# Two gated linear-attention blocks on one core: the ten sums of transposed x move from VectorE to GpSimd

## The chip, the core and the metric

The kernel runs on one core of a Trainium2 chip. A core has five engines with a queue of their own: TensorE (PE, with its weight loads shown as PEld), VectorE (DVE), ScalarE (ACT), GpSimd (POOL) and SyncE (SP), which here only issues DMAs. The metric is the device time of one execution in microseconds (us). The kernel before took 175.12 us, the median of three runs (174.89, 175.12, 175.48).

## What is computed

Two linear-attention blocks, A and B, read the same x (2048 x 640, bf16) and have their own weights. A gate mixes their results.

```python
H, Dh = 32, 20
qkv = x @ wqkv                       # 2048 x 1920, split into q, k, v
phi = lambda t: where(t > 0, t + 1, exp(t)) + 1e-6
kv = sum over s of phi(k)[s] v[s]^T  # per head, 20 x 20
z  = sum over s of phi(k)[s]         # per head, 20
o  = (phi(q) @ kv) / (phi(q) . z + 1e-6)
a, b = (o @ wo) of block A, of block B
g = sigmoid((x * gate_w).sum(-1))
out = g * a + (1 - g) * b
```

## The kernel before, in words

x stands in SBUF twice: as it is (`XN`, 16 tiles of 128 rows) and transposed (`XT`, five chunks of 128 features by 2048 rows). Tiles 0 and 1 are transposed by TensorE, the others by DMA transposes on SP's queue: tiles 2, 3, 4 and 5 alone, then 6 and 7, then 8 to 11, then 12 to 15.

The work has stages that follow one another on TensorE. First, phi(k) of both blocks for all 16 row tiles (stage K, tokens that begin with K in the list `MAIN`). Then G, products of phi(k) with x, from which k^T v is had without computing v. Then Q and R, phi(q) for the four blocks of 512 rows; small products that make one matrix per block out of kv and wo; and O, the output.

Many of these products of 2 x 2 blocks are made with seven block products in place of eight (a Strassen scheme): sums and differences of the operands are formed first, seven products are taken, and the results are combined. In stage K this is done for two pairs of row tiles, `KU = (3, 6,)`: unit 3 is x tiles 6 and 7, unit 6 is x tiles 12 and 13. Its functions:

- `kw_sums` forms four sums of the weights (`KW[1]` to `KW[4]`, lines about 774), on VectorE, once.
- `kx_sums(u)` forms five differences of transposed x for unit u: `KX[u, 1]` to `KX[u, 4]` have 128 partitions x 256 columns, `KX[u, 5]` has 128 x 128, all bf16. That is line 795, and there are ten in all. `KX[u, 2]` needs `KX[u, 1]`, and `KX[u, 4]` needs `KX[u, 2]`. All five need the two transposed tiles.
- `ks_unit(u)` holds the seven products (line 823 on TensorE). In the order of `MAIN` they are K3.1, K3.2, K3.5, K3.6, K3.7, K3.3, K3.4, with products of other tiles between them. Step 5 reads `KX[u, 1]`, step 6 `KX[u, 2]`, step 7 `KX[u, 3]`, and step 3 reads `KX[u, 4]` and `KX[u, 5]`. ScalarE saves two of the products (line 829), and VectorE adds them to others (lines 834 and 836).

Behind every k product, `k_post` makes phi: ScalarE takes the exponential (line 706) and the relu (lines 718, 733) out of PSUM, VectorE clamps the exponential (line 709) and adds the two (lines 724, 736), or does relu and sum in one (line 745). A two-bank piece of PSUM becomes free when these have read it, and TensorE can't begin the next product before that; there are eight banks. VectorE also forms the sums of phi(k) for stage G (`s_pair`, line 895) and of x (`t_all`, line 920). Later, the line 1003, 1029 sums serve stage Q, lines 1219 and 1233 stage G. GpSimd does some memsets at the start, four broadcasts of the gate (line 985) and the padding of wv (line 550).

The order on each engine is fixed before the run. The order of TensorE is written out by hand in `MAIN`. For the other engines, the class `Sched` plans: every operation has an engine, an assumed cost, the buffers it reads and writes, and a priority, and the planner takes on each engine the operation that can start first by these assumed costs, at equal start the one of lower priority number. The assumed costs have no other effect. What results is one queue for each engine, with semaphore waits where an operation needs another engine's (or an earlier own) result.

Of the kernel before, what the change touches and what calls it, by code (L numbers as in the profile page):

```python
# [113 lines left out]
class Sched:  # L114
# [9 lines left out]
    def op(self, eng, fn, cost, ins=(), outs=(), after=(), prio=None, name="", dma=None):  # L124
        if eng == "ACT" and dma is None:
            after = list(after) + self.consts
        o = Op(eng, fn, cost, list(ins), list(outs), after, (self.base or len(self.ops)) if prio is None else prio, name, dma)
        self.ops.append(o)
        return o
# [184 lines left out]
def body(nc, A_x, A_wqkv, A_wo, B_x, B_wqkv, B_wo, gate_w, out, log=None):  # L314
# [153 lines left out]
    def dve2(n):  # L468
        return 150 + 0.53 * n
# [312 lines left out]
    def kx_sums(u):  # L782
        t1, t2 = 256 * u, 256 * u + 128
        a11, a12, a21, a22 = [XT[:, c : c + 2, lo : lo + 128] for lo in (t1, t2) for c in (0, 2)]
        for k, in0, in1, need in (
            (1, a21, a22, ()),
            (2, a11, KX[u, 1], (1,)),
            (5, XT[:, 4, t1 : t1 + 128], XT[:, 4, t2 : t2 + 128], ()),
            (3, a21, a11, ()),
            (4, a12, KX[u, 2], (2,)),  # L790
        ):
            bkx[u, k] = Buf("kx")
            op(
                "DVE",
                lambda e, k=k, in0=in0, in1=in1: e.tensor_tensor(out=KX[u, k], in0=in0, in1=in1, op=ALU.subtract),
                dve2(128 if k == 5 else 256),
                ins=[bxt[2 * u], bxt[2 * u + 1]] + [bkx[u, j] for j in need],
                outs=[bkx[u, k]],
                name="kx",
            )  # L800
# [156 lines left out]
    for t in range(2, KT):  # L957
        k_both(t, "AB" if t in RELUB else "A")
        if t % 2:
            s_pair(t // 2)  # L960
        if t == KWT:
            kw_sums()
        for u in KU:
            if t == KXT[u]:
                kx_sums(u)
# [802 lines left out]
```

## Time and profile before

| | |
|---|---|
| median of three runs | 175.12 us |
| the profiled execution | 175.57 us |
| its span (first to last instruction) | 174.1 us |
| TensorE clock granted | 1.00 |
| busy: PE, DVE, ACT, POOL | 170.8, 142.5, 115.9, 4.9 us |
| stage K on TensorE | 3.75 to 47.3 us |
| stage G begins | 47.4 us |
| line 795, ten sums, 128x256 each 0.28 us, 128x128 each 0.22 us | five from 20.15 us, five from 30.08 us |

The page of the profile gives for each engine the busy time and its share of the span. The waits list who was idle and what ended it. The timeline lists instructions in order of their start: start in us, time in us, engine, line of the kernel, operation, output<-inputs, shapes, and, where several like ones follow one another, how many were merged. A queue's own row (SPq, ACTq) is the issue of a DMA, and the landing is told apart. Matmul ends are modelled, so a busy PE may still have small holes; the starts show them.

### The profile page before, as it was taken

Reading aid. Unit: us, or ns where it says so; the run is one execution under the profiler, and the core shown is the slowest. Engines: PE = TensorE matmul, PEld = TensorE weight load, DVE = VectorE, ACT = ScalarE, POOL = GpSimd, SP = SyncE. Lnnn points to the kernel's source line nnn. Section 1 sums busy time; section 2 is a strip of 40 time slices with the busy share of each in tenths; the row PEclk is TensorE's granted clock in tenths of the full one; section 3 lists DMA queues with packets and bytes.
Section 4 is the critical chain, followed back from the end, with each engine's and each line's share of the span. In section 5 each row is a group of like instructions: output and inputs, shape, how many; then the busy total and the mean of one; then the engine's idle time right before and its main releaser. Section 6 shows DMA issues by size and latency. Waiting matters only on the chain.

```text
span 174.1 us, 3381 instructions
## 1 busy us (share of the span) xinstructions
PE 170.8 (98%) x1327; PEld 107.3 (62%) x1327; DVE 142.5 (82%) x262; ACT 115.9 (67%) x225; POOL 4.9 (3%) x17
## 2 busy tenths in 40 slices
PE   9899999999999999999999999999999999999995
PEld 4455555555577776766555565655556677777773
DVE  2187999999999946948879989799999994999441
ACT  5369999999963323145998895766899773556423
POOL 2000000000000061000000000000000000000000
PEclk9999999999999999999999999999999999999999
DMA  6979999990000025329920003376842012460035
GB/s 185 302 146 152 203 324 367 357 223 18 4 0 0 0 41 98 75 49 188 235 65 0 4 2 62 76 204 150 269 114 82 0 38 79 92 218 4 0 111 191
DMA packets 33036, 20.59 MB, mean 118 GB/s; under 512 B 18261, under 2 KB 32893, under 8 KB 33021
## 3 DMA queue, kind: packets, MB, share of 16 engines
q1 hardware_dynamic: 32062, 19.76, 44.6%
q10 hardware_dynamic: 958, 0.63, 1.2%
q8 instruction: 10, 0.16, 0.4%
q14 instruction: 6, 0.04, 0.1%
HBM read 10.88 MB, written 4.26 MB: 87 GB/s over the span
## 4 chain that ended last, share of the span: by engine, by line
PE 96%; DMA 3%; SPq 0%; ACT 0%; issue 0%
PE ps L1184 22%; PE ps L1582 22%; PE ps L658 15%; PE ps L1056 13%; PE ps L1152 10%; PE ps L823 6%; PE ps L659 4%; DMA WKW<-in_A_wqkv_dram 3%; PE ps L1446 1%; PE ps L1372 1%; PE ps L1340 1%; SPq L451 0%; ACT PKS L1647 0%; PE ps L635 0%
## 5 line engine op out<-in xcount | busy, mean ns | idle before, releaser
L658 PE MATMUL ps<-WKW,XT 128*128 128x512 bf16 x120 | 33.9, 380 | 0.8 <-DMA WKW<-in_A_wqkv_dram 0.8
L659 PE MATMUL ps<-WKW,XT 128*128 128x128 bf16 (+1 forms) x120 | 26.3, 219 | 0.0
L1184 PE MATMUL ps<-TX,PKS 128*128 128x321 bf16 (+1 forms) x160 | 23.5, 300 | 0.0
L706 ACT ACTIVATE EKT<-ps 128x640 bf16<-128x640 f32 x30 | 20.8, 721 | 3.4 <-PE ps L659 3.0
L658 PEld LDWEIGHTS ps<-WKW,XT 128*128 128x128 bf16 x120 | 11.8, 98 | 15.1 <-DMA WKW<-in_A_wqkv_dram 1.1
L1184 PEld LDWEIGHTS ps<-TX,PKS 128*128 128x128 bf16 x160 | 15.6, 98 | 6.9 <-DVE DEN L1233 0.2
L1184 PE MATMUL ps<-XN,PKS 128*128 128x321 bf16 (+1 forms) x120 | 18.2, 300 | 0.0
L1184 PEld LDWEIGHTS ps<-XN,PKS 128*128 128x128 bf16 x120 | 11.7, 98 | 5.2
L895 DVE TENSOR_TENSOR PKS<-PKS 128x1280 bf16<-128x1280 bf16 (+2 forms) x20 | 12.9, 680 | 0.0
L718 ACT ACTIVATE PKS<-ps 128x640 bf16<-128x640 f32 x18 | 12.8, 724 | 0.0
L1214 ACT ACTIVATE EKT<-ps 128x321 f32<-128x321 f32 (+1 forms) x12 | 5.2, 438 | 11.2 <-PE ps L1184 5.6
L659 PEld LDWEIGHTS ps<-WKW,XT 128*128 128x128 bf16 x120 | 11.8, 98 | 0.0
L1088 ACT ACTIVATE EQ<-ps 128x512 bf16<-128x512 f32 x18 | 10.7, 604 | 1.5 <-PE ps L1056 1.0
L1163 ACT ACTIVATE EQ<-ps 128x1024 bf16<-128x1024 f32 x8 | 8.2, 1028 | 4.8 <-PE ps L1152 3.1
L709 DVE TENSOR_SCALAR EKT<-EKT 128x1280 bf16<-128x1280 bf16 (+1 forms) x20 | 8.2, 419 | 2.7 <-ACT EKT L706 2.7
L1056 PE MATMUL ps<-XT,WQA 128*128 128x512 bf16 x36 | 10.2, 379 | 0.0
L1065 ACT ACTIVATE PKS<-ps 128x512 f32<-128x512 f32 x12 | 7.0, 602 | 4.1 <-PE ps L1056 4.1
L1152 PE MATMUL ps<-XT,WQB 128*128 128x512 bf16 x40 | 9.4, 381 | 0.0
L1152 PE MATMUL ps<-XT,WQA 128*128 128x512 bf16 x40 | 9.3, 380 | 0.0
L1219 DVE TENSOR_TENSOR WKW<-ps,EKT 128x320 bf16<-128x320 f32 x12 | 5.8, 485 | 3.1 <-PE ps L1184 3.0
L724 DVE TENSOR_TENSOR PKS<-PKS,EKT 128x1280 bf16<-128x1280 bf16 x9 | 7.4, 817 | 0.1
L1605 DVE TENSOR_TENSOR PKS<-ps,EKT 128x320 bf16<-128x320 f32 x7 | 3.4, 491 | 4.7 <-PE ps L1582 2.7
(182 smaller groups left out, 338.7 us busy)
## 6 DMA issues: line engine op xcount, KB each, us to landing
out_dram<-PKS SPq DMA_DIRECT2D x15, 160.0 KB, 1.8
XN<-in_A_x_dram SPq DMA_DIRECT2D x1, 2240.0 KB, 9.5
WKW<-in_A_wqkv_dram SPq DMA_DIRECT2D x5, 160.0 KB, 4.3
WKW<-in_B_wqkv_dram SPq DMA_DIRECT2D x5, 160.0 KB, 4.1
WQA<-in_A_wqkv_dram SPq DMA_DIRECT2D x1, 800.0 KB, 11.1
WQB<-in_B_wqkv_dram SPq DMA_DIRECT2D x1, 800.0 KB, 12.3
WVA<-in_A_wqkv_dram SPq DMA_DIRECT2D x1, 800.0 KB, 12.4
PKS<-in_B_wqkv_dram SPq DMA_DIRECT2D x1, 800.0 KB, 5.0
```

Source lines behind the costliest of these rows:

```text
L658: e.matmul(a[:, 0:512], l, WK[X][:, c, 0:512], start=(c == 0), stop=(c == NC - 1))
L659: return e.matmul(a[:, 512:w], l, WK[X][:, c, 512:w], start=(c == 0), stop=(c == NC - 1))
L706: op("ACT", lambda e, i=i, ps=ps: e.activation(evg(i), psg(ps), ACT.Exp), act_cost(D), ins=[ps] + first, outs=[ek, b], name="ke")
L709: lambda e: e.tensor_scalar(EK[:, ek.slot : ek.slot + n, :], EK[:, ek.slot : ek.slot + n, :], 1.0, EPS, op0=ALU.min, op1=ALU.add),
L718: op("ACT", lambda e, X=X, ps=ps: e.activation(pkt(X, t), psg(ps), ACT.Relu), act_cost(D), ins=[ps], outs=[rk], name="kr")
L823: r = e.matmul(a[:, lo:hi], l, m[:, lo:hi], start=(first and i == 0), stop=(i == len(prs) - 1), skip_group_check=not first)
L895: lambda e: e.tensor_tensor(out=out, in0=a, in1=b, op=ALU.subtract),
L1056: r = e.matmul(PS[:, ps.slot, :], w, x, start=(first and i == 0), stop=(i == len(prs) - 1), skip_group_check=not first)
L1088: o = [op("ACT", lambda e: e.activation(EQ[:, eq.slot + h, :], pv(), ACT.Exp), act_cost(512), ins=ins, outs=[eq, ex], name="qe")]
L1152: r = e.matmul(PS[:, ps.slot + h, :], WQ[X][:, c, g::5], XT[:, c, 1024 + 512 * h : 1536 + 512 * h], start=(c == 0), stop=(c == NC - 1))
L1184: r = e.matmul(PS[:, ps.slot, 0:w], reg[:, j, :], mov(j, w), start=(first and j == 0), stop=(j == 7), skip_group_check=not first)
L1582: r = e.matmul(PS[:, ps.slot, 0:HALF], reg(g), mov(g), start=(first and g == 0), stop=(g == NC - 1), skip_group_check=not first)
```

## The change

In `kx_sums` the engine of the five differences is GpSimd ("POOL") in place of VectorE ("DVE"), and the assumed cost is 500 ns for 128 columns and 900 ns for 256, where the formula `dve2` gave 218 and 286 ns.

```diff
         ):
             bkx[u, k] = Buf("kx")
             op(
-                "DVE",
+                "POOL",
                 lambda e, k=k, in0=in0, in1=in1: e.tensor_tensor(out=KX[u, k], in0=in0, in1=in1, op=ALU.subtract),
-                dve2(128 if k == 5 else 256),
+                500.0 if k == 5 else 900.0,
                 ins=[bxt[2 * u], bxt[2 * u + 1]] + [bkx[u, j] for j in need],
                 outs=[bkx[u, k]],
                 name="kx",
```

Because the planner sees other costs and another engine, it lays out three queues anew. On GpSimd the ten differences stand behind the memsets of the start and ahead of line 985, in the order k = 1, 5, 2, 3, 4 for unit 3 and then the same for unit 6; the first waits for the DMA transpose of tiles 6 and 7, the sixth for that of tiles 12 to 15. On VectorE they are gone, and around their places line 895 sums come earlier (the fourth of the first four now ahead of line 834), line 836 comes directly behind line 834, and line 920 sums are grouped differently; up to about 62 us some line 895, 1003 and 1219 operations change places. On ScalarE one relu (line 733) stands two places later, and two exponentials (line 706) trade places with another. The orders of TensorE and of SP are the same instruction by instruction. TensorE's matmuls at K3.5, K3.6, K3.7 and K3.3 and their counterparts of unit 6 now wait for GpSimd's semaphore.

## The prediction

> **What bounds the kernel now.** I read the busy times of the page first, then the waits of PE, then the stages around the change, and last the single rows there.
>
> ```profile
> PE 170.8 (98%) x1327; PEld 107.3 (62%) x1327; DVE 142.5 (82%) x262; ACT 115.9 (67%) x225; POOL 4.9 (3%) x17
> ```
>
> PE computes for 170.8 of 174.1 us. The list of who waited for whom, for PE alone, says what is left:
>
> ```profile
> PE ps L658 <- DMA WKW<-in_A_wqkv_dram: 0.8, 1, 0.8
> PE ps L585 <- DVE ONE L483: 0.3, 1, 0.3
> ```
>
> Both waits are over at 5.34 us. Behind them PE runs without an idle time that the view counts; the only things I find in the timeline are 0.07 us before the matmul at 28.84 and about 0.1 us beyond an ordinary change of mode at 106.4. So what this change can save is at most some 0.2 us, and what it can lose is whatever makes PE wait. DVE decides that, as the busy times by stretch show (columns: PE, PEld, DVE, ACT, POOL, clock, DMA share, GB/s):
>
> ```profile
> 14.90:22.20 7.30, 7.30 (x56) 4.12 (x55) 7.16 (x15) 7.12 (x14) 0.00 (x0) 1.00 1.11 169
> 22.20:31.00 8.80, 8.80 (x66) 4.92 (x65) 8.62 (x18) 8.80 (x19) 0.00 (x0) 1.00 1.04 360
> 31.00:46.50 15.50, 15.50 (x116) 8.78 (x115) 15.33 (x26) 15.02 (x30) 0.00 (x0) 1.00 0.58 155
> 46.50:60.00 13.50, 13.50 (x101) 9.60 (x100) 13.38 (x26) 7.02 (x17) 0.00 (x0) 1.00 0.00 1
> ```
>
> From 15 to 60 us PE has no pause, and DVE is busy for 44.5 of the 45.1 us: two full engines side by side, PE just ahead as the bound. POOL does nothing there.
>
> **What is removed.** The ten sums stand in the view of line 795 and in DVE's timeline:
>
> ```profile
> L795 DVE TENSOR_TENSOR PQ<-XT x6: 215/280/284, 20.1 to 30.4; 128x256 bf16<-128x256 bf16 x4, 128x128 bf16<-128x128 bf16 x2
> L795 DVE TENSOR_TENSOR PQ<-XT,PQ x4: 281/282/285, 20.7 to 31.1; 128x256 bf16<-128x256 bf16 x4
> ...
> 20.15 0.62 DVE L795 TENSOR_TENSOR PQ<-XT 128x256 bf16<-128x256 bf16 x3
> 20.69 0.28 DVE L795 TENSOR_TENSOR PQ<-XT,PQ 128x256 bf16<-128x256 bf16 x1
> 20.89 0.81 DVE L895 TENSOR_TENSOR PKS<-PKS 128x1280 bf16<-128x1280 bf16 x1
> 21.62 0.28 DVE L795 TENSOR_TENSOR PQ<-XT,PQ 128x256 bf16<-128x256 bf16 x1
> ```
>
> From start to start the five sums of unit 3 hold DVE for 20.89 - 20.15 = 0.74 plus 21.83 - 21.62 = 0.21, together 0.95 us; those of unit 6 (30.08 to 30.82, 31.06 to 31.26) for 0.94 us. DVE is relieved of 1.9 us.
>
> **What GpSimd pays.** No row has a GpSimd sum of two tensors. The nearest is line 985, one input, also 128x256:
>
> ```profile
> L985 POOL TENSOR_SCALAR GSB<-GE x2: 842/1068/1293, 62.3 to 63.6; 128x256 bf16<-128x256 f32 x2
> L985 POOL TENSOR_SCALAR GSB<-GI x2: 842/842/842, 64.4 to 65.2; 128x256 bf16<-128x256 f32 x2
> ```
>
> Bounds for a 256-column sum: 0.28 us, DVE's own price (I have no row in which GpSimd beats DVE), and 1.68 us, the row twice, if the second input is read after the first. I take 0.84, the row itself, being the same engine and width; half, 0.42, for the two sums of 128 columns. A unit is 4 x 0.84 + 0.42 = 3.8 us.
> The Trainium skill ("GPSIMD Engine Reference", 3.1 Elementwise) gives 4.50 us for a two-input sum of 2048 fp32 columns; an estimate from it is 0.56 us for 256. With that the sum below would be 3.4 us in place of 4.7.
>
> **Is GpSimd in time?** Its queue takes them in the order k = 1, 5, 2, 3, 4. Unit 3 can begin when the transpose of x tiles 6 and 7 has landed: issued at 10.54, 4.5 us to landing, 15.0. PE asks for k=1 at 21.15, k=2 at 21.97, k=3 at 23.88, k=4 and 5 at 24.42. At the price taken they are ready at 15.8, 17.1, 17.9 and 18.8: at least 4.8 us early. A sum would have to cost (24.42 - 15.0) / 4.5 = 2.1 us before PE waited. Unit 6 (issue 16.71 + 5.5 = 22.2) is asked for at 37.56. Behind these sums in GpSimd's queue stand line 985 (62.3) and the padding of wv (83.2), far later. Alone, GpSimd hides them all.
>
> **Do the two engines disturb each other?** This is the term that decides. In 15 to 31 us DVE runs almost only sums of two SBUF tensors and clamps of exponentials, and one row has GpSimd beside such a sum:
>
> ```profile
> 62.13 0.76 DVE L1003 TENSOR_TENSOR WKW<-WQA,WKW 128x1280 bf16<-128x1280 bf16 x1
> 62.30 1.29 POOL L985 TENSOR_SCALAR GSB<-GE 128x256 bf16<-128x256 f32 x1 [61.02 <-DVE GI L976]
> ...
> 63.56 0.84 POOL L985 TENSOR_SCALAR GSB<-GE 128x256 bf16<-128x256 f32 x1
> ```
>
> The first of four equal instructions took 1.29 us, the other three 0.84. It began inside DVE's sum, which ended at 62.89, and it ended 63.59 - 62.89 = 0.70 us after that. This looks as if GpSimd stood still until DVE was done, all but 0.14 us of it. It might be a first-use cost, one row can't say; but beside line 1219 (one SBUF input, 65.09) neither engine is longer than usual. No row shows the opposite order, DVE coming second. I bound that: DVE waits for nothing (0), or for the 0.70 us that GpSimd needs undisturbed (0.35 for the short ones). I take the second, since the row shows exclusion and not sharing.
> The Trainium skill ("SBUF — State Buffer", Who interferes with whom) says the same and more: a DVE instruction with two SBUF inputs, or one in a two-port mode, and a GpSimd instruction that reads SBUF exclude each other for the whole instruction, whichever comes first. The row agrees for GpSimd second; by the rule DVE waits too.
>
> **The sum.** Per unit 4 x 0.70 + 0.35 = 3.15 us of waiting for DVE, two units 6.3. Unit 3's sums begin at 15.0 and lie among line 724, 774 and 709 work without a hole. Unit 6's begin at 22.2 or when unit 3's are done, and if DVE is late by then, they too come ahead of the combinations of unit 3 (lines 834 and 836), for which PE waits. The terms up to there:
>
> ```profile
> 23.70 0.81 DVE L724 TENSOR_TENSOR PKS<-PKS,EKT 128x1280 bf16<-128x1280 bf16 x1
> 24.62 0.83 DVE L834 TENSOR_TENSOR PQ<-ps,PQ 128x645 f32<-128x645 f32 x1
> 25.37 0.82 DVE L895 TENSOR_TENSOR PKS<-PKS 128x1280 bf16<-128x1280 bf16 x1
> ...
> 26.60 0.65 PE L823 MATMUL ps<-GSB,XT 128*128 128x512 bf16 x3
> ```
>
> - waiting of DVE: +6.3, less 0.1 in which DVE is idle anyway around 15.0
> - five sums gone: -0.95
> - the fourth line 895 sum now stands ahead of line 834, not behind it: +0.74 (25.37 to 26.10; ordered that way by the planner)
> - DVE's own idle time before line 834: -0.19 (24.43 to 24.62)
> - PE's spare time, line 834 done at 25.45 against the matmul at 26.60: -1.14
>
> 6.3 - 0.1 - 0.95 + 0.74 - 0.19 - 1.14 = +4.7 us. If only unit 3 lies ahead, it is 3.15 - 1.64 = +1.5 there, and unit 6 adds 3.15 - 0.94 = 2.2 in the stretch behind, where PE's spare time is used up (0.06 us at 28.84): +3.7. I take the middle, **+4.2**. Lost time isn't won back: PE is the bound from there to the end, and its order is unchanged. SP's queue is unchanged too; on ScalarE one relu moves two places back, at nothing, since ScalarE waits for the same PSUM; its cover is PE's delay, without which it could cost one relu, 0.7 us. The later shift of the TX sums (line 920) has its cover in PE's 192 products from 47.5 on.
>
> The profiled execution took 175.57 us (174.1 span and 1.47 around it), 0.45 above the median of 175.12. By the median: 175.12 + 4.2 = **179.3 us**. Ends: at 0.28 per sum, (0.14 held) x 9 = 1.3, less 1.64: no loss. At 1.68, 1.54 x 9 = 13.9, less 1.64: +12.2, 187.3. The range need not reach that far, as the price is nearest to the row of the same width.
>
> **Rivals.**
> - *No slower*: GpSimd and DVE don't exclude each other in the order that is new here, or GpSimd alone gives way. Then GpSimd's 4.8 us to spare hide the sums, DVE gains 1.9 us that nobody waits for, and the time is 175.1. For it: no row shows DVE held up. Against: the 1.29 us row. It decides as soon as the waiting of DVE up to line 834 stays under 1.64 us, about 0.2 us a sum instead of 0.70. Chance 0.20.
> - *A small loss*: DVE is held only for a part, 0.25 to 0.4 us a sum. 2.2 to 3.6 us less 1.64: 175.7 to 177. Chance 0.12.
> - *GpSimd starves*: DVE's sums follow one another so closely that GpSimd gets in only at the hole at 24.43. Then k=1 is ready at 15.8, but k=5 and k=2 at 24.43 + 0.42 + 0.84 = 25.7, and PE waits at its matmul of 21.97 for GpSimd: +3.7, 178.8. For it: DVE's starts lie 0.08 us ahead of the ends before them. Against: where DVE waits for itself (16.05) there are holes of 0.1. Chance 0.12.
> - *Faster*: the relief removes PE's last 0.2 us: 174.9, within what can't be told from no change (0.3%, 0.5 us). Over 0.5 us there is nothing to win behind 5.34. Chance 0.02.
> - *Far slower*: price near 1.68, or a pause of PE long enough for its clock to fall (the first matmuls, PE cold, start 0.43 us apart, 512 columns each; later a 512 and a 128 pass in 0.27). Over 183. Chance 0.04.
>
> **How the numbers follow.** The forecast case, DVE pushed back by 2 to 8 us net, 177 to 183, has 0.50. Slower by over 0.3%: 0.50 + 0.12 + 0.12 + 0.04 = 0.78; same 0.20; faster 0.02. Leaving out the unchanged case would leave out more than 2 in 10, so the range is 174.8 to 183.0; the likeliest case's own is 177 to 183.
>
> **What the profile after would show.** If right: line 795 on POOL from 15.0, single sums of 0.8 to 1.5 us; DVE's 0.82 us rows between 15 and 30 us at 1.2 to 1.6; PE waits between 23 and 35 us named after DVE or after ScalarE behind DVE, 3 to 6 us together; everything behind shifted by a constant. If GpSimd starves: PE waits for POOL at line 823, and DVE's rows keep 0.82. If nothing excludes: no PE wait, DVE rows unchanged, line 795 flat at its price. The forecast is wrong if the DVE rows are not longer while GpSimd runs, or if PE's order leaves more spare time before lines 834 and 836 than the 1.14 us I read.

## The result and the profile after

The changed kernel takes **179.50 us** (median of six executions, 178.50 to 179.70), the kernel before, beside it on the same chip, 175.18 us: a ratio of 1.0229, interval 1.0207 to 1.0251. It is 2.3% slower, 4.3 us. The profiled execution took 179.70 us with a span of 178.3 us; that of before had 175.57 and 174.1 us. Five of the six executions have a mean granted TensorE clock of 0.99 and lie between 179.48 and 179.70 us; the one with 1.00 took 178.50 us. So about 1.0 us of the 4.3 comes and goes with the clock.

The busy times and the clock row of the page of after:

```profile
PE 173.7 (97%) x1327; PEld 108.4 (61%) x1327; DVE 145.2 (81%) x252; ACT 116.1 (65%) x225; POOL 15.0 (8%) x27
PEclk9999998799999999999999999999999999999999
```

DVE has ten instructions fewer than before and is busy for 2.7 us longer: the sums have left it and it has more to do, not less. POOL's 10.1 us more are the ten sums. PE too is 2.9 us longer busy with the same instructions, and slices 7 and 8 of the clock row (27 to 36 us) are the only ones below 9. The waits of PE, complete:

```profile
PE ps L823 <- DVE PQ L834: 2.0, 1, 2.0
PE ps L585 <- DVE ONE L483: 0.3, 1, 0.3
PE ps L823 <- ACT PQ L829: 0.2, 1, 0.2
```

Two are new, and neither is for POOL. The long one is for the combination of unit 3 on VectorE, line 834, just the place where the prediction drew up its sum. The busy times by stretch, in the same four stretches as before (columns: PE, PEld, DVE, ACT, POOL, clock, DMA share, GB/s), and two of 3.41 us beside them:

```profile
14.90:22.20 7.30, 7.30 (x56) 4.15 (x54) 7.16 (x8) 6.96 (x13) 5.64 (x6) 1.00 1.18 183
22.20:31.00 8.80, 6.58 (x45) 3.31 (x43) 8.70 (x11) 5.50 (x12) 4.86 (x5) 0.95 1.05 365
31.00:46.50 15.50, 15.50 (x107) 8.62 (x106) 14.40 (x25) 14.94 (x29) 0.00 (x0) 0.92 0.56 147
46.50:60.00 13.50, 13.50 (x102) 8.92 (x101) 13.50 (x24) 8.89 (x20) 0.00 (x0) 1.00 0.01 2
26.69:30.10 3.41, 1.37 (x11) 0.62 (x9) 3.41 (x5) 0.85 (x3) 0.37 (x1) 1.00 1.07 365
30.10:33.51 3.41, 3.41 (x15) 1.69 (x14) 3.29 (x7) 3.41 (x7) 0.00 (x0) 0.50 1.08 352
```

In the first stretch DVE is as full as before (7.16 us) but gets through 8 instructions in place of 15; in the second it is busy for 8.70 us with 11 in place of 18. Five and four of the missing ones are the sums themselves; the others come later. PE stands in the second stretch for 2.2 us. The last line shows what comes on top: from 30.1 us on, PE runs 3.41 us at half its clock. Why DVE is slow is told by its timeline (start, time, instruction; the rows up to line 834 that matter):

```profile
15.26 1.27 DVE L724 TENSOR_TENSOR PKS<-PKS,EKT 128x1280 bf16<-128x1280 bf16 x1
16.64 0.86 DVE L774 TENSOR_TENSOR GSA<-WKW 128x1282 bf16<-128x1282 bf16 x1
17.42 1.30 DVE L774 TENSOR_TENSOR GSB<-WKW 128x1282 bf16<-128x1282 bf16 x1
18.63 1.29 DVE L774 TENSOR_TENSOR GSA<-GSA,WKW 128x1282 bf16<-128x1282 bf16 x1
19.84 0.96 DVE L709 TENSOR_SCALAR EKT<-EKT 128x1280 bf16<-128x1280 bf16 x1
20.72 0.82 DVE L774 TENSOR_TENSOR GSB<-WKW,GSA 128x1282 bf16<-128x1282 bf16 x1
...
26.46 1.28 DVE L724 TENSOR_TENSOR PKS<-PKS,EKT 128x1280 bf16<-128x1280 bf16 x1
27.67 0.81 DVE L895 TENSOR_TENSOR PKS<-PKS 128x1280 bf16<-128x1280 bf16 x1
28.40 0.82 DVE L834 TENSOR_TENSOR PQ<-ps,PQ 128x645 f32<-128x645 f32 x1
```

and by GpSimd's, in the same time:

```profile
15.18 0.67 POOL L795 TENSOR_TENSOR PQ<-XT 128x256 bf16<-128x256 bf16 x1 [13.89 <-DMA XT<-in_A_x_dram]
...
17.99 1.25 POOL L795 TENSOR_TENSOR PQ<-XT 128x256 bf16<-128x256 bf16 x1
...
25.82 1.25 POOL L795 TENSOR_TENSOR PQ<-XT,PQ 128x256 bf16<-128x256 bf16 x1
```

The first sum begins before DVE's line 724 and takes 0.67; line 724, 0.08 us behind it, takes 1.27 in place of 0.82. From then on the two alternate: where they meet, a DVE sum takes up to 1.30 and a GpSimd sum up to 1.25, and line 774 at 20.72, which meets none, takes 0.82 again. Line 834 starts at 28.40; before it was 24.62. The last GpSimd sum ends at 27.06, ahead of it.

These 3.78 us of lateness add up from the rows, each start against that of before: nine longer rows 3.9, DVE 0.14 late when it begins, 0.1 lost in a gap, the line 895 sum that now stands ahead 0.74, less the five sums of unit 3, 0.95, and less the idle time at 24.43, 0.19. PE, start against start: 0.14 behind at first, 0.33 more at K3.7 (24.35 for 23.88), 2.21 more at the matmul behind line 834 (29.28 for 26.60), 1.61 more by 33.52, where it runs at half its clock, and from there to the end a constant lag of 4.1 to 4.3. The span is 4.2 us longer.

### The profile page after: what moved, and what is told of

The parts are those of the page before. It is cut to its first block, busy times and chain, and to the rows that moved or that the text cites. A ratio compares the mean times of both kernels' runs of the same rounds, so it can differ in the third digit from the quotient of the medians.

```text
span 178.3 us, 3384 instructions
## 1 busy us (share of the span) xinstructions
PE 173.7 (97%) x1327; PEld 108.4 (61%) x1327; DVE 145.2 (81%) x252; ACT 116.1 (65%) x225; POOL 15.0 (8%) x27
## 4 chain that ended last, share of the span: by engine, by line
PE 88%; DVE 8%; ACT 3%; issue 0%; ACTq 0%; DVEq 0%
PE ps L1184 21%; PE ps L1582 21%; PE ps L1056 13%; PE ps L658 10%; PE ps L1152 10%; PE ps L823 3%; PE ps L659 3%; DVE PKS L895 2%; DVE PKS L724 2%; ACT EKT L706 1%; PE ps L585 1%; PE ps L1446 1%; DVE EKT L709 1%; PE ps L1372 1%; PE ps L1340 1%; DVE GSA L774 1%
## 5 line engine op out<-in xcount | busy, mean ns | idle before, releaser
L658 PE MATMUL ps<-WKW,XT 128*128 128x512 bf16 x120 | 36.6, 402 | 0.0
L659 PE MATMUL ps<-WKW,XT 128*128 128x128 bf16 (+1 forms) x120 | 27.3, 227 | 0.0
L658 PEld LDWEIGHTS ps<-WKW,XT 128*128 128x128 bf16 x120 | 12.3, 102 | 15.8 <-issue 2.4
L895 DVE TENSOR_TENSOR PKS<-PKS 128x1280 bf16<-128x1280 bf16 (+2 forms) x20 | 13.9, 731 | 0.1
L659 PEld LDWEIGHTS ps<-WKW,XT 128*128 128x128 bf16 x120 | 12.3, 103 | 0.0
L709 DVE TENSOR_SCALAR EKT<-EKT 128x1280 bf16<-128x1280 bf16 (+1 forms) x20 | 9.2, 467 | 2.9 <-ACT EKT L706 2.9
L724 DVE TENSOR_TENSOR PKS<-PKS,EKT 128x1280 bf16<-128x1280 bf16 x9 | 8.3, 922 | 0.1
L1647 ACT ACTIVATE PKS<-ps 128x320 bf16<-128x320 f32 x8 | 3.5, 437 | 6.3 <-PE ps L1582 6.3
```

What stands on the lines that cost most here:

```text
L658: e.matmul(a[:, 0:512], l, WK[X][:, c, 0:512], start=(c == 0), stop=(c == NC - 1))
L659: return e.matmul(a[:, 512:w], l, WK[X][:, c, 512:w], start=(c == 0), stop=(c == NC - 1))
L709: lambda e: e.tensor_scalar(EK[:, ek.slot : ek.slot + n, :], EK[:, ek.slot : ek.slot + n, :], 1.0, EPS, op0=ALU.min, op1=ALU.add),
L724: return e.tensor_tensor(out=v, in0=v, in1=EK[:, ek.slot : ek.slot + 2, :].rearrange("p x (g m) -> p (x g) m", g=NC), op=ALU.add)
L895: lambda e: e.tensor_tensor(out=out, in0=a, in1=b, op=ALU.subtract),
```

## The experiments

The theory: a GpSimd sum that reads SBUF and a DVE instruction that adds two SBUF tensors, or clamps one, exclude each other; a sum costs DVE up to half a microsecond, and PE, which has hardly any spare time, loses what DVE is late. The rivals: the new order on DVE and ScalarE, or PE's new waits for GpSimd, cost the time; GpSimd is simply too slow; or the lost clock is the cause and not a consequence. Every time below is the median of its runs and stands against the runs of the kernel before on the same chip (175.39 us for the run in which GpSimd reads nothing, the two with one unit alone and the one with unit 6 later; 175.53 for the two with additional GpSimd sums of x; 175.48 for the other four).

### Same orders, same waits, GpSimd reads nothing

```diff
-                lambda e, k=k, in0=in0, in1=in1: e.tensor_tensor(out=KX[u, k], in0=in0, in1=in1, op=ALU.subtract),
+                lambda e, k=k: e.memset(KX[u, k], 0.0),
```

> All queues in the order of the changed kernel, and the same waits, but GpSimd writes zeros in the ten places (a memset) and reads nothing, so the seven-product tiles are computed from zeros. Exclusion theory (a GpSimd sum that reads SBUF and a DVE instruction with two SBUF inputs or a clamp shut each other out): the reading is gone, the DVE rows between 15 and 30 us are back at 0.82 us, PE has no wait at line 823, time 175.1 us (174.8 to 175.5). Rival, order (the new order on DVE and ScalarE and the waits of PE for GpSimd cost the time): nothing of that has changed, so 179 us or near it. Rival, slow GpSimd (sums late for PE): a memset is short, so 175 us too, but then PE's waits in the changed kernel should have been named after GpSimd.

175.29 us, ratio 0.9992 (0.9978 to 1.0007). The whole loss is gone. GpSimd's row, and two of DVE's:

```profile
L795 POOL MEMSET PQ<- x10: 204/311/316, 15.2 to 23.4; 128x256 bf16 x8, 128x128 bf16 x2
```

```profile
16.93 0.83 DVE L774 TENSOR_TENSOR GSB<-WKW 128x1282 bf16<-128x1282 bf16 x1
24.76 0.83 DVE L834 TENSOR_TENSOR PQ<-ps,PQ 128x645 f32<-128x645 f32 x1
```

GpSimd writes the same buffers from the same place in its queue (15.2 us on), PE has the same semaphores to wait for, DVE and ScalarE the orders of the changed kernel, and line 834 is back at 24.76. So the new orders, the waits of PE for GpSimd and writing alone cost nothing, and DVE's relief of ten sums brings nothing: PE was the bound. What remains is that GpSimd reads, or that it is slow and its results come late. The next run takes out the second.

### The ten sums as additional work in the kernel before

```diff
-    bgt, gtx = Buf("gtx"), []
+    [op("POOL", lambda e, i=i, u=u, w=w: e.tensor_tensor(out=TXf[:, 256 * i : 256 * i + w], in0=XT[:, 0, 256 * u : 256 * u + w], in1=XT[:, 1, 256 * u : 256 * u + w], op=ALU.subtract), 900.0, ins=[bxt[2 * u], bxt[2 * u + 1]], outs=[bxo], name="extra") for i, (u, w) in enumerate([(u, w) for u in KU for w in (256, 128, 256, 256, 256)])]; bgt, gtx = Buf("gtx"), []
```

> The kernel before with its queues as they are, DVE's ten sums included; GpSimd makes ten sums of the same sizes in addition (of other columns of the same transposed tiles), from the landing of tiles 6 and 7 and of tiles 12 to 15 on, into memory that is free until 39 us. It is the disturbance alone: no relief of DVE, no new order, no wait of PE for GpSimd. Exclusion theory: 3.7 us of lateness (8 x 0.47) ahead of line 834, not made smaller by removed sums; PE's loss is DVE's lateness, less at most 0.2 us: 178.5 to 180, like the changed kernel or somewhat more. If GpSimd waits instead of DVE wherever DVE has no pause (as the first sum of unit 6 did when unit 6 was on GpSimd alone, 2.99 us): part of the ten sums stand still and the loss is below 2 us. Rival, order: 175.3.

179.69 us, ratio 1.0235 (1.0211 to 1.0260). DVE still makes its ten sums, in the order of before, nobody uses what GpSimd makes, and the loss is 4.2 us. PE's waits:

```profile
PE ps L823 <- DVE PQ L795: 2.3, 2, 1.6
PE ps L658 <- ACT EKT L706: 1.0, 1, 1.0
```

Here the sums of line 795 themselves are late, on DVE, since they stand behind rows of 1.05 to 1.30 us and are held up too; line 834 starts at 28.77. No one waits for a result of GpSimd, so its speed can't be the cause: it is its presence beside DVE. That the loss has the same size as in the changed kernel is chance in part: here DVE is 4.14 us late behind the combinations, since no sum has left it, and the clock of the profiled execution stays at 1.00; in the changed kernel it is 3.16 us late there, and the clock adds about 1.0.

### What a GpSimd sum costs alone

Ten sums of the same shapes, on weights, at 3.5 to 9.5 us in the kernel before, when DVE has little to do:

```diff
-    warm(5)
+    [op("POOL", lambda e, i=i, w=w: e.tensor_tensor(out=TXf[:, 256 * i : 256 * i + w], in0=WK["A"][:, 0, 0:w], in1=WK["A"][:, 0, 320 : 320 + w], op=ALU.subtract), 900.0, ins=[bwk["A", 0]], outs=[bwz]) for i, w in enumerate((256, 256, 256, 128) * 2 + (256, 256))], warm(5)
```

> The kernel before, and ten more GpSimd sums of two SBUF tensors (eight of 128x256 bf16, two of 128x128, on weights) from about 3.5 us on, when DVE has little to do; nobody needs their results but the weight sums of line 774, at 16 us, wait until they are done. It measures the disputed price by itself. Exclusion theory with the hold that the changed kernel showed (DVE rows 0.46 to 0.48 us longer): alone a sum takes 0.8 to 0.9 us, of which 0.46 shuts DVE out; DVE rows of line 709 and 724 beside them get longer, the rows of line 745 and 615 (one input from PSUM, at most one from SBUF) don't. Rival, price: alone 1.25 us, the length of the rows in the changed kernel, so that the 1.25 there is GpSimd's own and not waiting. Time: 175.2 us, all hidden, if they are done by 15 us.

175.31 us, ratio 0.9989 (0.9975 to 1.0003). GpSimd, three of the ten:

```profile
3.54 0.67 POOL L936 TENSOR_TENSOR TX<-WKW 128x256 bf16<-128x256 bf16 x1 [2.26 <-DMA WKW<-in_A_wqkv_dram]
...
5.42 0.42 POOL L936 TENSOR_TENSOR TX<-WKW 128x128 bf16<-128x128 bf16 x1
...
8.83 0.66 POOL L936 TENSOR_TENSOR TX<-WKW 128x256 bf16<-128x256 bf16 x1
```

and DVE beside them:

```profile
8.38 0.82 DVE L745 SCALAR_TENSOR_TENSOR PKS<-ps,EKT 128x640 bf16<-128x640 f32 x1
9.12 0.56 DVE L709 TENSOR_SCALAR EKT<-EKT 128x640 bf16<-128x640 bf16 x1
```

A sum of 256 columns costs 0.67 us undisturbed, below the 0.8 to 0.9 expected, and one of 128 costs 0.42: by these two widths, 1.95 ns a column and 0.17 us fixed. Line 745, with one input in PSUM and one in SBUF, keeps its 0.82 beside a GpSimd sum. Line 709, one SBUF input in bf16, does not: 0.56 for 0.33.

### GpSimd reads one input in place of two

```diff
-                lambda e, k=k, in0=in0, in1=in1: e.tensor_tensor(out=KX[u, k], in0=in0, in1=in1, op=ALU.subtract),
+                lambda e, k=k, in0=in0: e.tensor_scalar(KX[u, k], in0, 1.0, None, op0=ALU.add),
```

> Like the changed kernel, but each of the ten GpSimd operations reads one input and adds 1 (a tensor_scalar), so the seven-product tiles are computed from other numbers. Exclusion theory, the hold being the reading of two inputs one after the other: hold halved to 0.23 us for 256 columns, DVE rows at 1.05 us in place of 1.28, about 1.9 us of DVE waiting ahead of line 834 in place of 3.7; PE's wait there about 0.5 us and no low clock: 176 to 177.5 us. If the hold is the writing or the whole instruction, it stays at 0.46 and the time at 179.5.

175.94 us, ratio 1.0024 (1.0014 to 1.0035), just below what was expected. GpSimd, the first alone and one of those beside DVE:

```profile
15.85 0.85 POOL L795 TENSOR_SCALAR PQ<-XT 128x256 bf16<-128x256 bf16 x1 [14.57 <-DMA XT<-in_A_x_dram]
...
17.29 1.18 POOL L795 TENSOR_SCALAR PQ<-XT 128x256 bf16<-128x256 bf16 x1
```

DVE:

```profile
17.68 1.02 DVE L774 TENSOR_TENSOR GSA<-GSA,WKW 128x1282 bf16<-128x1282 bf16 x1
...
25.79 0.82 DVE L834 TENSOR_TENSOR PQ<-ps,PQ 128x645 f32<-128x645 f32 x1
```

This operation holds GpSimd longer (0.85 alone, 1.0 to 1.35 beside DVE) and DVE less: its rows are 0.91 to 1.02, 0.1 to 0.2 us more than alone, where the two-input sum of 0.67 costs them 0.47. Line 834 is 1.2 us late instead of 3.8. How long DVE is shut out is not the length of the GpSimd instruction. The run changes the operation along with the number of inputs, so it doesn't show that the second input alone makes the difference.

### One unit alone, and unit 6 later

Against the kernel before, the five sums of one unit on GpSimd, the queues laid out anew for that (the second run has 6 for 3):

```diff
-                "DVE",
+                "POOL" if u == 3 else "DVE",
...
-                dve2(128 if k == 5 else 256),
+                (500.0 if k == 5 else 900.0) if u == 3 else dve2(128 if k == 5 else 256),
```

Against the changed kernel, unit 6's sums held back until unit 3's line 834 is done:

```diff
-    bkw, bkx = {}, {}
+    bkw, bkx, kx_op = {}, {}, {}
...
-            op(
+            kx_op[u, k] = op(
...
-                comb(pz, s2, False)
+                o = comb(pz, s2, False); [j == 3 and kx_op[6, k].deps.append(o) for k in range(1, 6)]
```

> Only the five sums of unit 3 on GpSimd, those of unit 6 on DVE; the planner lays out the queues for that. Exclusion theory: 2.1 us of DVE waiting ahead of line 834, less the five sums removed; PE's wait about 0.6 us, no low clock: 175.4 to 176.3 us. If each unit costs one half of the whole: 177.3. If the whole comes from unit 3: 179.5.

> Only the five sums of unit 6 on GpSimd, from 22.2 us, those of unit 3 on DVE. Exclusion theory: five x 0.46 = 2.1 to 2.3 us of DVE waiting between 22 and 28 us, nothing removed ahead of line 834, 0.19 us of idle time there and 1.14 us to spare: PE waits 0.8 us, no low clock, 175.6 to 176.5 us. If each unit costs one half: 177.3. The sum of the gains over before of this and of unit 3 alone would be about 1.5 us against 4.3 for both, since PE's spare time swallows the first 1.3 us twice and the clock doesn't fall.

> All queues in the order of the changed kernel; one wait more: GpSimd begins the five sums of unit 6 only when line 836 of unit 3 is done, so that only unit 3's sums lie ahead of line 834. Exclusion theory: about five sums x 0.46 us = 2.1 to 2.3 us of DVE waiting ahead of line 834 in place of 4.2, PE's wait there falls from 2.2 us to about 0.6, no low clock behind it; the other five push DVE back later by about 2 us, which is 1 to 2 us of PE in small waits. 176.3 to 177.7 us. If the later five find spare time: 175.7. Rival, order: unchanged, 179.5 us. Rival, slow GpSimd: unit 6 even later, 179.5 or more.

Unit 3 alone: 177.29 us, 1.0113 (1.0098 to 1.0128). Unit 6 alone: 175.62, 1.0016 (1.0000 to 1.0033). Unit 6 later: 178.14, 1.0155 (1.0137 to 1.0174).

The first and the third take more than expected of them, and their waits say why. PE, unit 3 alone:

```profile
...
PE ps L823 <- ACT PQ L829: 0.4, 1, 0.4
PE ps L658 <- ACT EKT L706: 0.4, 1, 0.4
...
PE ps L1184 <- DVE PKS L724: 0.2, 1, 0.2
...
```

PE, unit 6 later:

```profile
PE ps L658 <- ACT PKS L733: 0.7, 1, 0.7
PE ps L823 <- ACT PQ L829: 0.4, 1, 0.4
PE ps L658 <- ACT EKT L706: 0.4, 1, 0.4
...
PE ps L823 <- ACT ps L848: 0.3, 1, 0.3
...
```

With unit 3 alone line 834 starts at 26.25, 1.63 us late. PE lags only 0.53 us there, as its spare time leads one to think, but 1.99 us at the start of stage G: the rest follows in small waits, most of them for ScalarE; that ScalarE is late there because it stands behind DVE is argued. The spare time put the loss off and did not take it away. It is the same with unit 6 held back: line 834 at 26.44, and 2.8 us in the end; there unit 6's sums hold up DVE further behind line 834.

Unit 6 alone is another case. Its first sum:

```profile
21.46 2.99 POOL L795 TENSOR_TENSOR PQ<-XT 128x256 bf16<-128x256 bf16 x1 [20.18 <-DMA XT<-in_A_x_dram]
```

It stood for 2.3 us more than its price while DVE's rows kept their 0.81. Line 834 of unit 3 started at 24.04, so little was lost. The last run below looks at that.

### DVE late with GpSimd out of it

Against the kernel before, five (or three) additional sums on DVE, directly ahead of line 834, of two SBUF inputs each:

```diff
     span = sch.run()
+    at = next(i for i, o in enumerate(sch.order) if o.name == "kcm")
+    for i in range(5):
+        d = Op("DVE", lambda e, i=i: e.tensor_tensor(out=TXf[:, 1280 * i : 1280 * i + 1280], in0=WK["A"][:, 0:2, 0:D], in1=WK["B"][:, 0:2, 0:D], op=ALU.subtract), 740.0, [], [], [], 0, "dum", None)
...
+        sch.order.insert(at, d)
```

> The kernel before with all ten sums on DVE and GpSimd idle; DVE gets five extra sums of 128x1280 right ahead of line 834, into memory that is free then. It puts the same lateness on DVE without any GpSimd. 5 x 0.74 = 3.7 us: line 834 starts at about 28.1, PE waits 28.1 + 0.83 + 0.06 - 26.6 = 2.4 us. If the low clock of the changed kernel comes from PE's pause alone, it comes here too: 3.4 us at half clock, 1.7 us more, 179 to 179.6 us in all. If it doesn't come: 177.5 us.

> The same with three extra sums, 2.2 us: line 834 starts at about 26.7, PE waits 0.9 us there and no low clock follows; some small waits behind it as with unit 3 alone: 176.1 to 177.4 us. If a pause of 0.9 us lowers the clock too: 177.8 or more.

Five: 179.04 us, 1.0198 (1.0164 to 1.0233). Three: 177.27, 1.0101 (1.0082 to 1.0119). The row of line 834 with five, and PE behind it:

```profile
28.28 0.82 DVE L834 TENSOR_TENSOR PQ<-ps,PQ 128x645 f32<-128x645 f32 x1
29.16 0.72 PE L823 MATMUL ps<-GSB,XT 128*128 128x512 bf16 x4 [2.23 <-DVE PQ L834]
```

The stretches of 3.41 us there:

```profile
26.46:29.87 3.41, 1.18 (x9) 0.56 (x8) 3.41 (x6) 0.73 (x2) 0.00 (x0) 1.00 1.07 372
29.87:33.28 3.41, 3.41 (x15) 1.62 (x13) 3.34 (x7) 3.41 (x8) 0.00 (x0) 0.50 1.08 363
```

Without any work for GpSimd, DVE as late as in the changed kernel gives the same pause of PE (2.2 us) and the same half clock behind it. So the clock follows from PE's pause and needs no GpSimd. The four executions took 179.54 and 179.61 us at a mean clock of 0.99, and 178.45 and 178.54 at 1.00: 1.1 us apart, like the executions of the changed kernel. With three, 2.2 us of additional work cost 1.8 us, and PE's waits are

```profile
PE ps L658 <- ACT EKT L706: 1.0, 1, 1.0
PE ps L823 <- DVE PQ L834: 0.8, 1, 0.8
```

so here too the spare time only divides the loss between two places.

How late DVE is behind both combinations can be compared over all runs at one instruction, the first line 709 of 640 columns there, which starts at 27.97 in the kernel before. The profiled executions don't all begin alike: at 20 us, before PE has met any of this, PE lies up to 0.6 us ahead of the one of before or up to 0.3 behind, and DVE with it. So the table has, for each profiled execution, the lateness of DVE there, PE's lag at 20 and at 60 us, all against the profiled execution of before, and beside them the time lost by the medians:

| run | DVE's lateness there | PE's lag at 20 us | PE's lag at 60 us | time lost |
|---|---|---|---|---|
| GpSimd reads nothing | -0.39 us | 0.14 us | 0.06 us | -0.1 us |
| unit 6 alone | 0.27 | -0.59 | -0.10 | 0.2 |
| five additional GpSimd sums (below) | 0.45 | -0.57 | 0.02 | 0.5 |
| one input | 0.54 | -0.10 | 0.69 | 0.5 |
| unit 3 alone | 1.01 | -0.35 | 1.99 | 1.9 |
| unit 6 later | 1.56 | -0.17 | 2.79 | 2.8 |
| three additional sums on DVE | 1.70 | -0.31 | 1.69 | 1.8 |
| five additional sums on DVE | 3.65 | 0.17 | 4.17 | 3.0 (clock 1.00), 4.1 (0.99) |
| ten additional GpSimd sums | 4.14 | 0.26 | 4.13 | 4.2 |
| the changed kernel | 3.16 | 0.14 | 4.29 | 3.3 (clock 1.00), 4.3 (0.99) |

Both counted from 20 us on, the two runs in which line 834 itself is on time are 0.86 and 1.02 us late there and lose 0.49 and 0.59: some 0.4 us of PE's spare time is a real discount. In the others that are late PE loses all of it. Two lose about a microsecond more, besides the two with the half clock. With unit 6 later, DVE is held up again behind that instruction; with unit 3 alone, 0.65 of the extra 1.0 us comes up after 39 us, where GpSimd does nothing, and its cause stays open.

### Can GpSimd be kept out?

Five additional sums on GpSimd in the kernel before, like the ten above, but held back until VectorE has made its own last sum of unit 3. So they begin at 21.4 us, when DVE works through rows that follow one another closely. Against the kernel with ten:

```diff
...
-    ins=[bxt[2 * u], bxt[2 * u + 1]], outs=[bxo], name="extra") for i, (u, w) in enumerate([(u, w) for u in KU for w in (256, 128, 256, 256, 256)])]
+    ins=[bkx[3, 4]], outs=[bxo], name="extra") for i, (u, w) in enumerate([(3, 256)] * 5)]
```

> The kernel before, and five extra GpSimd sums of 128x256 that begin when DVE has made the last difference of unit 3 (at 21.9 us), in a stretch in which DVE's instructions follow one another without a pause until about 24.4 us. If GpSimd gets the memory only in a pause of DVE: the first of the five takes about 2.5 to 3 us, until the pause ahead of line 834, no DVE row before that is longer, and the other four alternate with DVE from there: 1.4 to 1.9 us of lateness behind line 834, time 176 to 177.2 us. If the one who has waited longest goes first: the first takes at most 1.25 us, DVE rows from 22 us on at 1.28, lateness ahead of line 834 about 1.4 us, and the time is 176.5 to 177.7 us. The length of the first GpSimd row tells them apart.

176.00 us, 1.0024 (1.0010 to 1.0039). GpSimd:

```profile
21.42 3.05 POOL L969 TENSOR_TENSOR TX<-XT 128x256 bf16<-128x256 bf16 x1 [20.14 <-DVE PQ L795]
```

DVE in the same time:

```profile
21.25 0.81 DVE L895 TENSOR_TENSOR PKS<-PKS 128x1280 bf16<-128x1280 bf16 x1
...
23.13 0.81 DVE L724 TENSOR_TENSOR PKS<-PKS,EKT 128x1280 bf16<-128x1280 bf16 x1
24.05 0.83 DVE L834 TENSOR_TENSOR PQ<-ps,PQ 128x645 f32<-128x645 f32 x1
24.80 0.98 DVE L895 TENSOR_TENSOR PKS<-PKS 128x1280 bf16<-128x1280 bf16 x1
```

The sum stands through four rows of DVE (21.25, 21.99, 22.39 and 23.13), each of which starts 0.07 to 0.08 us before the end of the one ahead of it, and none is longer than alone. DVE's first pause is 23.94 to 24.05. The sum ends at 24.47, 0.53 us behind the start of that pause, which is most of its 0.67. From there on the two alternate, and DVE's rows are longer (0.98, 0.95, 1.18).

But a pause is not the whole condition. With unit 3 alone the first GpSimd sum also came second, beside the DVE row at 15.70, and the next DVE row started 0.08 us before the end of that one:

```profile
15.99 1.06 POOL L795 TENSOR_TENSOR PQ<-XT 128x256 bf16<-128x256 bf16 x1 [14.71 <-DMA XT<-in_A_x_dram]
```

```profile
15.70 0.83 DVE L774 TENSOR_TENSOR GSA<-WKW 128x1282 bf16<-128x1282 bf16 x1
16.45 1.30 DVE L774 TENSOR_TENSOR GSB<-WKW 128x1282 bf16<-128x1282 bf16 x1
```

The sum got in without a pause, 1.06 us long, and the second DVE row was held up. One of the ten additional sums did the same (22.02, 0.92 us, between DVE's rows at 21.61 and 22.34). What decides between getting in and standing is open, so leaving no pause is no sure way to keep GpSimd out.

## Why the prediction was right

The forecast was 179.3 us and the result 179.50. The mechanism is the one it named, exclusion in both orders. That the number is only 0.2 us off is luck: the waiting was 2.3 us too large, a discount of 1.14 was hardly to be had, about 1.0 for the clock was missing, the middle of two branches was taken where the larger one came, and these nearly cancelled.

- **PE is the bound, so the relief of DVE brings nothing:** right. The run in which GpSimd reads nothing has the relief without the cost, and takes 175.29.
- **GpSimd is in time:** right. PE has no wait for POOL in the profile of after.
- **The price, 0.84 us:** mis-sized (it enters the sum only through the time held). 0.67 for 256 columns, 0.42 for 128 (that one was met). The row it came from, line 985, has one input, and the one-input form turns out to be the slower (0.85 with bf16 too). The bound that took a second input for a second read was far off. The 3.4 us that stands beside the price of 0.56 takes the whole of it as held; the other sums take the price less 0.14, and by that it would be 0.42 x 9 - 1.64 = 2.1.
- **They exclude each other, also with DVE second:** right, and this decides. Line 724 at 15.26 is the missing row. The Trainium skill ("SBUF — State Buffer", Who interferes with whom) has a vector instruction with two SBUF inputs contend with a GpSimd instruction that reads SBUF and not with one that only writes it; the pair of runs with reading (179.50) and writing alone (175.29) agrees, and so does line 745 with its one SBUF input at 0.82. Its "for the whole instruction" does not agree: DVE loses 0.47 to a sum of 0.67, and 0.1 to 0.2 to a one-input operation of 0.85. Line 709, with one SBUF input, is held up too (0.56 for 0.33); whether it runs in a two-port mode, which the prediction's rule has as well, no run here shows.
- **Held for 0.70 a sum:** mis-sized, 0.47. With it DVE's waiting ahead of line 834 is 3.9 us where the sum had 6.2, and line 834 starts at 28.40 where the sum puts it at 24.62 + 5.8 = 30.4.
- **The other terms** (the sums gone, the line 895 sum moved, the idle time) have the sizes forecast; with 3.9 in place of 6.2 they give 3.5, and with the 0.14 and 0.1 at the beginning the 3.8 measured. Both units' sums came ahead of line 834, the first of the two branches between which the forecast took the middle.
- **PE's spare time, less 1.14:** wrong as a term. At the matmul behind line 834 it is there (3.78 of lateness, 2.68 of lag), but the table of lateness and loss shows that PE in the end loses what DVE is late behind the combinations, less at most some 0.4. DVE, before the change busy for 28.7 of the 29.0 us from 31 to 60, doesn't catch up.
- **The clock:** not in the sum, only in the rival named far slower. PE loses 1.61 us where it is at half clock. What that is worth in the end is less, the 1.0 to 1.1 us between executions with and without it; that DVE's lateness would have cost the remainder in any case is argued from the small waits of the other runs.

So the sum with measured sizes is 3.2 us of DVE's lateness behind the combinations, with no discount, and in most executions 1.0 for the clock: 4.2. The forecast had 2.3 us too much of waiting, a discount of 1.14 that was not to be had, and no clock. The signs it named came: DVE's rows at 1.27 to 1.30 (1.2 to 1.6 said), line 795 at 0.67 to 1.25 (0.8 to 1.5), everything behind shifted by a constant; PE's waits, 2.2 us in the list and 2.5 by the starts, stay under the 3 to 6.

Of the rivals, "GpSimd starves" is a real behaviour (2.99 and 3.05 us for a sum of 0.67) and did not happen here. The first sum came at 15.18, before a DVE row; but others came second and got in all the same, the first one of unit 6 in the changed kernel in a pause of 0.04 us (22.27 to 22.31). "No slower" fell with the first longer DVE row.

What stays open: why GpSimd mostly takes its turn after the DVE row beside which it starts, though DVE's rows then follow one another as closely as those that kept it out for 2.3 us. And no version found beats the kernel before: the best, the one without reads, leaves out what the sums are for and only ties.

## What to carry to other kernels

Before an almost idle engine is given work, ask what it shares with the engine that is relieved: here ten sums worth 1.9 us of DVE came off it and cost it 3.9. If the bound engine and its helper are both full, a spare time of the bound engine in front of one wait is hardly a discount (0.4 us of 1.14 here); count the helper's lateness nearly whole. And if the loss comes as one pause of TensorE, add the clock.

## What the runs showed that was not expected

- A two-input subtraction on GpSimd (0.67 us, 128x256 bf16) is faster than adding a constant to one input (0.85), and it keeps DVE out for 0.47 against 0.1 to 0.2.
- GpSimd can stand for 2.3 us beside a DVE that leaves no pause, and then get in at one of 0.11 us; but it also got in between DVE rows without a pause.
- A pause of PE of 2.0 to 2.2 us is followed by half a clock over the next 3.41 us in both traces that have one. Pauses of 1.6, 0.7 and 1.0 us, in the trace with ten additional GpSimd sums, left it at 1.00, though two other executions of that kernel have 0.99. In the trace of after the clock is full for 23.89 us (seven times 3.41) and then half for 3.41; with five sums more on DVE it is full for 23.89 and half for 3.41 again. In the 3.41 us before the drop PE was busy for 1.37 and 1.18 us. This looks like windows of 3.41 us, each judged by how busy PE was, so that the same pause may fall into one or be split between two; the executions of one kernel with and without the loss fit that, but no run moved the pause to try it. The Trainium skill ("TensorE: Matmul & The Clock Gate", Part 1: The HAM clock gate) gives the same free-running window and asks for an idle one before the drop; here PE was busy for 40% of the 3.41 us before the drop.
